# Block-sorted attention and FFN on one core: v sorted and loaded in another order, spread matrices in bf16, a third bank for the first FFN chunk

## The chip, the cores and the metric

The kernel runs on one NeuronCore of a Trainium2 chip. The engines of a core work side by side and are kept in step by semaphores: PE (TensorE, matrix products; its weight loads are shown as PEld), DVE (VectorE), ACT (ScalarE), POOL (GpSimd) and SP (SyncE). In this kernel POOL and SP do little but issue DMAs, POOL the loads that turn f32 into bf16 and SP the rest; 16 DMA engines carry them out. The metric is the time of one execution on the device in microseconds (us).

## The reference

Inputs: q, k and v of 4 batches, 8 heads, 768 positions and 64 dimensions, a sort_net of one 8x8 matrix for each batch and head, and two FFN weights (512x2048 and 2048x512) with 2048 slopes alpha.

```python
P = sort_net
for _ in range(5):                     # Sinkhorn
    P = exp(P - max(P, -1))
    P = P / (sum(P, -1) + 1e-9);  P = P / (sum(P, -2) + 1e-9)
k_sorted = einsum('bhij,bhjcd->bhicd', P, k in 8 blocks of 96)
v_sorted = einsum('bhij,bhjcd->bhicd', P, v in 8 blocks of 96)
attn = softmax(q_block @ k_sorted_block.T / 8)      # in each block of 96
x = (attn @ v_sorted_block) as (3072 tokens, 512)
h = x @ w_in
out = (max(h, 0) + alpha * min(h, 0)) @ w_out
```

So P mixes whole blocks of k and v, attention stays within a block, and each token then goes through the FFN.

## The kernel before

**Tiling.** A block of 96 positions of one batch, all 8 heads, is one step of `attention(g, ...)`; there are 32, g = 8b + i. A step is: scores (L596 for batch 0, L593 for the others), their maximum on DVE (L600), transposed scores with the maximum subtracted (L624 or L614, with L606), the exponential on ACT (L634), the product with v (L642), normalization on DVE (L647, L650), a transposition on PE (L659) and a copy into `xT` (L320, the line of all plain copies). The FFN goes over chunks of tokens, 192 for the first two and 384 for the others: `ffn1` makes 16 groups of 128 hidden rows for a chunk, each four matmuls (L679), drained by ACT (L687) and DVE (L690) into `hT`; `ffn2` makes 128 tokens of output in four parts of four matmuls (L711), and SP sends them out (L721).

**Sorting.** The sort is a product with a block-diagonal "spread" matrix, made from P on PE and DVE: `spread_k` (L446 to L454) makes BDK for a batch, `spread_v` (L461 to L469) makes BDV for two. Each starts with an f32 matmul of a selection matrix with P and ends in three DVE instructions. `prep_k` (L484) sorts k into `KT`. v of batch 0 is sorted by L526. v of the later batches is sorted by `sort_v` (L548): 12 products of 512 columns into one PSUM bank, each copied to `VD`; batch 1 is done alone, batches 2 and 3 in pairs. `turn_v` then sends `VD` to DRAM (L559) and fetches it back turned (L566), in two halves for each batch, into `VS[b % 2]`, which L642 reads. q of batches 1 to 3 is loaded in eight DMAs (L346) into `QN` and turned by six DMA transposes on SP (L353) into `QTz[b % 2]`.

**Buffers that tie steps together.** There is one `QN`, so the loads of the next q wait for the turns of the last one. `VST` has two halves: v2 goes where v0 was, and v3 where v1 was, so the load of v3 waits for the twelfth sort of v1. `KS`, `KT`, `QTz` and `VS` have two buffers each.

**Order.** Nothing is ordered by hand. Each operation is put in a graph with what it reads and writes, a duration and a priority (lower is more urgent). `schedule` simulates the five queues with its own costs (L131 to L143: for a DMA, how long it holds its issuing engine, and when it lands) and fixes each engine's order; `emit` writes this order out with the waits. An engine works strictly in that order: what stands behind a waiting instruction waits too. A priority says which of the ready operations is listed first, and the planner's costs decide what it takes to be ready. `fill` puts extra matmuls, whose result nobody reads, on PE where the planner sees it idle (L819), before the first use of their bank.

POOL's order before, behind the early loads and weights: k1, q1, k2, v1, v2, q2, q3, v3, k3. SP's order before, around q2: six turns of q2, send of half 0 of v1 (L559), an output, fetch of half 0 (L566), an output, send of half 1, fetch of half 1, then the sends of v2 and v3.

Of the kernel before, what the change touches and what calls it, by code (L numbers as in the profile page):

```python
# [7 lines left out]
AP = bass.AP  # L8
ACTF = mybir.ActivationFunctionType
BF16 = mybir.dt.bfloat16  # L10
# [46 lines left out]
class _Graph:  # L57
# [30 lines left out]
    def schedule(self):  # L88
# [31 lines left out]
        while done < len(ops):  # L120
# [14 lines left out]
            if op.dma is not None:  # L135
                free[e] = at + (600 if e == "pool" else 100)
                begin = max(dma_free if e == "pool" else 0, free[e] + 700)
                if e == "pool":
                    dma_free = begin + dur
                op.end = begin + dur + (2500 if e == "pool" else 500)  # L140
            else:
                op.end = free[e] = at + dur
# [11 lines left out]
    def fill(self, make, unit, first, before):  # L154

        out, last = [], self.ops[first].end + 300
        for op in self.order["pe"]:
            n = int((op.start - max(last, 5000)) * 0.9 / unit)
            if op.start < before and n > 0:
                x = _Op("pe", lambda e, n=n: make(e, n), n * unit, 0.0, None, len(self.ops))  # L160
                x.start, x.end = max(last, 5000), max(last, 5000) + n * unit
                x.deps.add(first)
                self.ops.append(x)
                out.append(x)
            out.append(op)
            last = max(last, op.end)
# [72 lines left out]
def bass_sinkhorn_attn__then__act_prelu_kernel(  # L239
# [29 lines left out]
    P32 = sb("P32", [32, 64], F32)  # L269
    rm = sb("rm", [32, 8], F32)  # L270
# [6 lines left out]
    selk = sb("selk", [32, 4, 128], F32)  # L277
    selv = sb("selv", [32, 2, 128], F32)
    dtmp = sb("dtmp", [128, 64], F32)
    dsel = sb("dsel", [128, 8], F32)  # L280
# [96 lines left out]
    def consts():  # L377
# [15 lines left out]
        def red(o, src, w):  # L393
# [10 lines left out]
        G.add(DVE, lambda e: e.tensor_copy(AP(VS[0], 64, [[64 * 65, 112], [65, 64]]), AP(one0, 0, [[1, 112], [0, 64]])),  # L404
              200, r=["one0"], w=[("VS1", 0)], prio=-70)
# [14 lines left out]
    def sinkhorn():  # L420
# [4 lines left out]
        for it in range(5):  # L425
# [11 lines left out]
            if it == 0:  # L437
# [3 lines left out]
            dv(lambda e: e.tensor_tensor(out=P3T, in0=P3T, in1=bc(cs), op=AluOpType.mult),  # L441
               ["P", "cs"], ["P"])

    def spread_k(b, prio):
        after = [] if b == 0 else [("xT", 1)]
        G.add(PE, lambda e: e.matmul(psYP[:, 1, 0:64], AP(selk, b * 128, [[512, 32], [1, 128]]),  # L446
                                     P32[:, :]), 500, r=["P", "selk"] + after, w=PSP, prio=prio)
        G.add(DVE, lambda e: e.tensor_tensor(
            out=AP(dtmp, 0, [[64, 128], [8, 8], [1, 8]]), in0=AP(psYP, 512, [[1024, 128], [8, 8], [1, 8]]),
            in1=AP(mkj, 0, [[8, 128], [0, 8], [1, 8]]), op=AluOpType.mult), 210,  # L450
            r=PSP + ["mkj"], w=["dtmp"], prio=prio)
        G.add(DVE, lambda e: e.reduce_sum(dsel[:, :], AP(dtmp, 0, [[64, 128], [8, 8], [1, 8]]),
                                          axis=AxisListType.X), 200, r=["dtmp"], w=["dsel"], prio=prio)
        G.add(DVE, lambda e: e.tensor_tensor(  # L454
            out=AP(BDK, b * 128, [[512, 128], [16, 8], [2, 8], [1, 2]]),
            in0=AP(mkh, 0, [[16, 128], [2, 8], [0, 8], [1, 2]]),
            in1=AP(dsel, 0, [[8, 128], [0, 8], [1, 8], [0, 2]]), op=AluOpType.mult), 260,
            r=["dsel", "mkh"], w=[("BDK", b)], prio=prio)

    def spread_v(x, prio):  # L460
        G.add(PE, lambda e: e.matmul(psYP[:, 1, 0:64], AP(selv, x * 128, [[256, 32], [1, 128]]), P32[:, :]),  # L461
              500, r=["P", "selv", ("xT", 1)], w=PSP, prio=prio)
        G.add(DVE, lambda e: e.tensor_tensor(
# [398 lines left out]
```

## Time and profile before

| | |
|---|---|
| runs, us | 303.24, 303.05, 301.84 (median 303.05) |
| the profiled execution | 301.19, with a span of 299.5 |
| PE busy from 150 us to the end | 146.35 of 149.5 us |
| loads of k, v (each, median) | 23.7 and 24.4 us from issue to landing |
| fetches of sorted v, six halves | 6.8 to 14.0 us from issue to landing |
| sends of sorted v, six halves | 3.7 to 13.3 us |
| first use of v2 and v3 on PE | 108.65 us |
| first L642 of batch 1 | 116.49 us |

The span begins with the first instruction and ends with the last; the execution's time is a little longer. In the profile's lines, L548 is a line of the kernel before. A line of the timeline is: start, duration, engine, source line, operation, what is written from what, how many; in brackets how long the engine was idle before it, and what ended that. A line of the waits is: engine and line, what it waited for, total, times, longest. PE's clock is granted by the hardware, in these rows at full or half speed.

### The profile page before, as it was taken

To read this page: it belongs to the slowest core of one execution; us is meant where nothing else is said; L and a number is where in the kernel's file an instruction comes from. 1 tells how busy PE (TensorE), PEld (TensorE's weight loads), DVE (VectorE), ACT (ScalarE), POOL (GpSimd) and SP (SyncE) were. 2 spreads that over 40 slices of the span, in tenths; PEclk is the share of its full clock that TensorE was granted. 3 is DMA by queue.
4 is the path that set the end of the run, shared out by engine and by line. 5 is a ranking of instruction groups with operands and counts; after the bars stand their busy time and mean duration, and the time that the engine had idled before them with its cause. 6 is when DMAs were issued, how large, how long until landed. Compare 5 with 4: busy or idle time off the path is not lost.

```text
span 299.5 us, 6232 instructions
## 1 busy us (share of the span) xinstructions
PE 267.3 (89%) x2705; PEld 167.4 (56%) x2705; DVE 173.2 (58%) x351; ACT 134.8 (45%) x259; POOL 35.0 (12%) x53
## 2 busy tenths in 40 slices
PE   5996999999960049999999999999999999999995
PEld 1575877663440026656666666666666666655542
DVE  6795665763760007767766666776666566654410
ACT  4384225664530016456556445434444544444421
POOL 8990000017046000000000000000000000000000
PEclk9997559999995559999999999999999999999999
DMA  6999999999899995496689940100101000100111
GB/s 121 207 206 189 215 169 214 177 166 105 129 189 88 188 191 27 125 73 155 40 131 149 64 84 35 38 2 35 37 35 37 11 27 35 37 35 35 37 70 70
DMA packets 65691, 29.78 MB, mean 99 GB/s; under 512 B 57136, under 2 KB 61248, under 8 KB 65472
## 3 DMA queue, kind: packets, MB, share of 16 engines
q0 software_dynamic: 24112, 13.63, 37.3%
q1 hardware_dynamic: 41552, 15.75, 36.6%
q8 instruction: 21, 0.34, 0.5%
q14 instruction: 6, 0.05, 0.1%
HBM read 29.64 MB, written 8.65 MB: 128 GB/s over the span
## 4 chain that ended last, share of the span: by engine, by line
PE 79%; DMA 7%; DVE 5%; SPq 2%; POOL 2%; ACT 2%; issue 1%; POOLq 0%
PE psH L679 27%; PE psYP L711 24%; DMA VST<-in_v_dram 5%; PE psS L606 4%; PE psO L642 4%; PE psS L711 3%; PE psS L593 3%; PE psS L614 3%; PE psYP L548 2%; SPq L353 2%; POOL QN L346 2%; PE psO L659 2%; PE psYP L484 2%; DMA QTz<-QN 1%; PE psS L624 1%
## 5 line engine op out<-in xcount | busy, mean ns | idle before, releaser
L690 DVE SCALAR_TENSOR_TENSOR hT<-t,omaT,psH 128x384 bf16<-128x384 f32 (+1 forms) x144 | 80.3, 566 | 79.7 <-ACT t L687 78.9
L679 PE MATMUL psH<-xT,w_in_bf 128*128 128x384 bf16 (+1 forms) x576 | 104.1, 317 | 0.6 <-DVE hT L690 0.5
L687 ACT ACTIVATE t<-psH 128x384 f32<-128x384 f32 (+1 forms) x144 | 64.6, 453 | 70.1 <-PE psH L679 69.4
L711 PE MATMUL psYP<-w_out_bf,hT 128*128 128x512 bf16 x336 | 87.0, 383 | 0.4 <-DVE hT L690 0.4
L679 PEld LDWEIGHTS psH<-xT,w_in_bf 128*128 128x128 bf16 x576 | 51.2, 101 | 28.3 <-DVE hT L690 2.7
L711 PEld LDWEIGHTS psYP<-w_out_bf,hT 128*128 128x128 bf16 x336 | 30.9, 98 | 29.0 <-issue 2.1
L634 ACT ACTIVATE Esb<-psS 96x768 bf16<-96x768 f32 (+1 forms) x31 | 25.0, 807 | 23.7 <-PE psS L606 23.1
L600 DVE TENSOR_REDUCE nm<-psS 96x8 bf16<-96x768 f32 x31 | 29.4, 950 | 2.1 <-PE psS L593 0.7
L548 PE MATMUL psYP<-VST,BDV 64*64 64x512 bf16 x36 | 9.9, 413 | 21.1 <-DMA VST<-in_v_dram 20.8
L346 POOL DMA_DIRECT2D QN<-in_q_dram x24 | 20.4, 887 | 57.6 <-DMA QTz<-QN 57.6
L606 PE MATMUL psS<-identb,nm 96*96 96x96 bf16 (+1 forms) x248 | 23.6, 215 | 0.0
L606 PEld LDWEIGHTS psS<-identb,nm 96*96 96x96 bf16 (+1 forms) x248 | 21.6, 130 | 2.3
L320 ACT ACTIVATE VD<-psYP 64x512 bf16<-64x512 f32 (+1 forms) x14 | 8.3, 594 | 30.3 <-PE psYP L548 30.1
L650 DVE TENSOR_TENSOR xq<-psO,rec 96x512 bf16<-96x512 f32 x31 | 21.3, 686 | 1.0
L642 PEld LDWEIGHTS psO<-VS,Esb 96*96 96x96 bf16 (+1 forms) x248 | 16.0, 129 | 5.7 <-ACT Esb L634 0.5
L614 PE MATMUL psS<-QTz,KT 128*96 128x192 bf16 x96 | 18.5, 248 | 0.1
L320 ACT ACTIVATE outstg<-psYP 128x512 f32<-128x512 f32 x21 | 12.5, 597 | 10.0 <-PE psYP L711 10.0
L642 PE MATMUL psO<-VS,Esb 96*96 96x65 bf16 (+1 forms) x248 | 16.7, 213 | 0.4 <-ACT Esb L634 0.2
L548 PEld LDWEIGHTS psYP<-VST,BDV 64*64 64x64 bf16 x36 | 2.5, 104 | 25.7 <-DMA VST<-in_v_dram 21.0
L819 PE MATMUL psYP<-identb 128*128 128x512 bf16 x32 | 10.5, 476 | 3.3 <-ACT identb L320 3.3
L614 PEld LDWEIGHTS psS<-QTz,KT 128*96 128x96 bf16 x96 | 11.9, 124 | 2.7 <-DVE nm L600 0.2
L593 PEld LDWEIGHTS psS<-KT,QTz 128*96 128x96 bf16 x192 | 11.5, 125 | 2.8
(112 smaller groups left out, 196.3 us busy)
## 6 DMA issues: line engine op xcount, KB each, us to landing
out_dram<-outstg SPq DMA_DIRECT2D x24, 256.0 KB, 2.0
KS<-in_k_dram POOLq DMA_DIRECT2D x4, 768.0 KB, 23.7
VST<-in_v_dram POOLq DMA_DIRECT2D x4, 768.0 KB, 24.4
QN<-in_q_dram POOLq DMA_DIRECT2D x24, 96.0 KB, 11.7
v_sorted_dram<-VD SPq DMA_DIRECT2D x6, 384.0 KB, 5.0
VS<-v_sorted_dram SPq DMA_DIRECT2D x6, 384.0 KB, 10.4
w_in_bf<-in_moe_w_in_dram POOLq DMA_DIRECT2D x4, 512.0 KB, 17.0
w_out_bf<-in_moe_w_out_dram POOLq DMA_DIRECT2D x2, 1024.0 KB, 27.3
```

The source lines that it names most:

```text
L320: return e.activation(o, i, ACTF.Copy) if e is nc.scalar else e.tensor_copy(o, i)
L346: G.add(POOL, lambda e, h=h: e.dma_start(AP(QN, h * 128 + (h // 4) * 64, [[6144, 128], [1024, 6], [1, 64]]), AP(q.tensor, b * HB + h * S * ...
L600: G.add(DVE, lambda e: e.tensor_reduce(AP(nm[m], 0, [[8, 96], [4, 2], [1, 4]]), AP(psX, 0, [[1024, 96], [512, 2], [96, 4], [1, 96]]), Axis ...
L606: return e.matmul(AP(psX, (p // 4) * 512 + (p % 4) * 96, [[1024, nk], [1, 96]]), AP(nm[m], p, [[8, 96], [0, nk]]), AP(identb, 0, [[128, 96 ...
L614: e.matmul(AP(psX, (h4 // 2) * 512 + (h4 % 2) * 192, [[1024, 96], [1, 192]]), AP(KT[n], (h4 * 8 + i) * 96, [[ld, 128], [1, 96]]), AP(QTz[n ...
L634: G.add(ACT, lambda e: e.activation(AP(Esb[m], 0, [[768, nk], [384, 2], [1, 384]]), AP(psX, 0, [[1024, nk], [512, 2], [1, 384]]), ACTF.Exp ...
L642: inst = e.matmul(AP(psZ, hp * 512 + h4 * 68, [[1024, 96], [1, 65]]), AP(Esb[m], pos(h4, hp) * 96, [[768, nk], [1, 96]]), AP(VS[n], ((hp * ...
L650: G.add(DVE, lambda e: e.tensor_tensor(out=AP(xq[m], 0, [[512, 96], [256, 2], [64, 4], [1, 64]]), in0=AP(psZ, 0, [[1024, 96], [512, 2], [6 ...
L679: inst = e.matmul(AP(psH, hb * 512, [[1024, 128], [1, n]]), AP(w_in_bf, kt * DFF + ft * 128, [[KT_TILES * DFF, 128], [1, 128]]), AP(xT, kt ...
L687: G.add(ACT, lambda e: e.activation(AP(t1[tb], 0, [[384, 128], [1, n]]), AP(psH, hb * 512, [[1024, 128], [1, n]]), ACTF.Relu, scale=-1.0), ...
L690: G.add(DVE, lambda e: e.scalar_tensor_tensor(out=AP(hT, ft * RING + tok % RING, [[FT_TILES * RING, 128], [1, n]]), in0=AP(t1[tb], 0, [[38 ...
L711: inst = e.matmul(AP(bank[0], bank[1], [[row, 128], [1, 512]]), AP(hT, ft * RING + tok % RING, [[FT_TILES * RING, 128], [1, 128]]), AP(w_o ...
```

## The change

1. The planner's DMA costs: a DMA on POOL holds it for 700 instead of 600 ns, a transposing DMA holds SP for 1300 instead of 100, and DMAs on SP of 1000 ns or more land 1000 ns later than before.
2. The sorts of v have priority 8b - 1 (they had 8b + 2 and more). For batch 1 they, and k's sorts, are listed with the last three blocks of batch 0. The load of v3 gets priority 8b - 18.5 in place of 8b - 17; q2's is 8b - 18.
3. `spread` takes the place of `spread_k` and `spread_v`. The last Sinkhorn step writes P in bf16 (`Pb`), the selection matrices are bf16, and behind batch 0's matrix the three others for k and both for v come from five matmuls into one bank, two DVE products, one reduction and four DVE products.
4. FFN1 of the first chunk (192 tokens) rotates over three PSUM banks, the third being the one that spread matrices and sorts use.
5. `fill` may also put its extra matmuls between the first FFN1 group and the first FFN2 part.
6. The ones column of `VS[0]` is copied by ACT instead of DVE, and the scores of block 2 wait for the normalization of block 1.

What this does to the queues: POOL's order becomes k1, q1, k2, v1, v2, q2, v3, first load of q3, k3, the other seven of q3. SP's order around q2 becomes: two outputs, send of half 0 of v1, a turn, an output, a turn, fetch of half 0, two turns, send of half 1, two turns, fetch of half 1, sends of v2 and v3. For q3: two turns, both fetches of v3, four turns. PE gets four filler matmuls in two pairs ahead of the first FFN2 part, and one more at the start. The twelve sorts of v1 stay spread between FFN groups, and the first sort of v2 and v3 has two more FFN1 groups ahead of it and the first scores of batch 1 behind it.

```diff
@@ schedule
-                free[e] = at + (600 if e == "pool" else 100)
+                free[e] = at + (700 if e == "pool" else 1300 if op.dur == 2500 else 100)
...
-                op.end = begin + dur + (2500 if e == "pool" else 500)
+                op.end = begin + dur + (2500 if e == "pool" else 500 if op.dur < 1000 else 1500)
@@ fill
-    def fill(self, make, unit, first, before):
+    def fill(self, make, unit, first, spans):
...
+            for lo, hi in spans:
+                begin = max(last, lo)
+                n = int((op.start - begin) * 0.9 / unit)
+                if op.start <= hi and n > 0:
...
-    G.fill(warm, 215, ident_op, first_y[0].start)
+    G.fill(warm, 215, ident_op, [(5000, first_y[0].start), (ffn_ops[0].start + 1, ffn_ops[1].start)])
@@ constants and Sinkhorn
-    selk = sb("selk", [32, 4, 128], F32)
-    selv = sb("selv", [32, 2, 128], F32)
+    selk = sb("selk", [32, 4, 128], BF16)
+    selv = sb("selv", [32, 2, 128], BF16)
...
-        G.add(DVE, lambda e: e.tensor_copy(AP(VS[0], 64, [[64 * 65, 112], [65, 64]]), AP(one0, 0, [[1, 112], [0, 64]])),
-              200, r=["one0"], w=[("VS1", 0)], prio=-70)
+        G.add(ACT, lambda e: copy(e, AP(VS[0], 64, [[64 * 65, 112], [65, 64]]), AP(one0, 0, [[1, 112], [0, 64]])),
+              220, r=["one0"], w=[("VS1", 0)], prio=-60)
...
+            o = AP(Pb, 0, [[64, 32], [1, 8], [8, 8]]) if it == 4 else P3T
+            dv(lambda e, o=o: e.tensor_tensor(out=o, in0=P3T, in1=bc(cs), op=AluOpType.mult),
+               ["P", "cs"], ["Pb" if it == 4 else "P"])
@@ spread in place of spread_k and spread_v
+    def spread(bs, vs, prio):
+        nk, nv = len(bs), len(vs)
+        after = [("xT", 1)] if vs else []
+
+        def f(e):
+            inst = None
+            for x in range(nk + nv):
+                sel = AP(selk, bs[x] * 128, [[512, 32], [1, 128]]) if x < nk else \
+                    AP(selv, vs[x - nk] * 128, [[256, 32], [1, 128]])
+                inst = e.matmul(psYP[:, 1, x * 64:x * 64 + 64], sel, Pb[:, :])
+            return inst
+        G.add(PE, f, 100 * (nk + nv), r=["Pb", "selk", "selv"] + after, w=PSP, prio=prio)
...
@@ attention
-        G.add(PE, s1, t_pe(*[(96, 96)] * 8), r=kt_keys + qt_keys, w=banks_s, prio=ps_)
+        G.add(PE, s1, t_pe(*[(96, 96)] * 8), r=kt_keys + qt_keys + [("xq", 1)] * (g == 2),
+              w=banks_s, prio=ps_)
@@ ffn1
-        hb, tb = step[0] % 2, step[0] % 3
+        tb = step[0] % 3
+        pt, poff, _, keys = (BANK_H + [BANK_P])[step[0] % 3] if ga < 2 else BANK_H[step[0] % 2]
@@ the main loop
-                load_v(3, 8 * b - 17)
+                load_v(3, 8 * b - 18.5)
...
-            for x in range(1, 4):
-                spread_k(x, x)
-                if x < 3:
-                    spread_v(x - 1, x)
+            spread([1, 2, 3], [0, 1], 1)
...
-                if i == 1 + x * 7 // len(units):
+                if i == (5 + x * 3 // len(units) if b == 0 else 1 + x * 7 // len(units)):
                     f, *a = units[x]
+                    pr = 8 * b + 2 + x * 5 / len(units)
                     if f is None:
-                        turn_v(b + 1, a[1], 8 * b + 2 + x * 5 / len(units))
+                        turn_v(b + 1, a[1], 8 * b - 1)
+                    elif f is sort_v:
+                        f(*a, 8 * b - 1)
                     else:
-                        f(*a, 8 * b + 2 + x * 5 / len(units))
+                        f(*a, pr)
```

## The prediction

> **What bounds the kernel now.** First the page's slices, for where TensorE (PE) is not full:
>
> ```profile
> span 299.5 us, 6232 instructions
> ...
> PE 267.3 (89%) x2705; PEld 167.4 (56%) x2705; DVE 173.2 (58%) x351; ACT 134.8 (45%) x259; POOL 35.0 (12%) x53
> ...
> PE   5996999999960049999999999999999999999995
> ...
> PEclk9997559999995559999999999999999999999999
> DMA  6999999999899995496689940100101000100111
> ```
>
> A slice is 7.5 us. PE is full except at the start and in slices 12 to 14, where the DMA engines are full instead. From there on PE alone sets the pace. The waits, then PE, POOL and SP in order of time, say what the hole is:
>
> ```profile
> PE psYP L548 <- DMA VST<-in_v_dram: 20.8, 1, 20.8
> ```
> ```profile
> 87.28 0.52 PE L593 MATMUL psS<-KT,QTz 128*96 128x96 bf16 x8
> 108.65 0.63 PE L548 MATMUL psYP<-VST,BDV 64*64 64x512 bf16 x2 [20.84 <-DMA VST<-in_v_dram]
> ```
> ```profile
> 66.15 6.62 POOL L346 DMA_DIRECT2D QN<-in_q_dram  x8 [43.73 <-DMA QTz<-QN]
> 86.66 6.56 POOL L346 DMA_DIRECT2D QN<-in_q_dram  x8 [13.89 <-DMA QTz<-QN]
> 93.14 0.62 POOL L371 DMA_DIRECT2D VST<-in_v_dram  x1
> ```
> ```profile
> 75.47 8.86 SPq L353 DMA_TRANSPOSE QTz<-QN  x6
> ...
> 89.05 0.34 SPq L566 DMA_DIRECT2D VS<-v_sorted_dram  x1
> ...
> 94.26 0.45 SPq L559 DMA_DIRECT2D v_sorted_dram<-VD  x1
> 107.56 0.34 SPq L566 DMA_DIRECT2D VS<-v_sorted_dram  x1
> ```
>
> (start, duration, work, idle before it.) PE stands 20.84 us at the first sort of v2 and v3, because v3 was issued only at 93.14: POOL's queue had q3 ahead of it, q3 (86.66) waited for the six turns of q2, and these (75.47) for q2's loads (66.15). Last, the granted clock by stages:
>
> ```profile
> 30.00:45.00 15.00, 15.00 (x116) 11.56 (x116) 9.74 (x30) 4.27 (x11) 0.00 (x0) 0.55 1.61 192
> ...
> 93.00:108.60 15.60, 0.00 (x0) 0.00 (x0) 0.00 (x0) 0.00 (x0) 1.34 (x3) 0.50 2.22 155
> ```
>
> The first number after the comma is PE's busy time, the third from the end the clock. It is half from 26.4 to 43.5 although PE is busy, and from 91.3 to 111.8 because of the hole.
>
> **v3's place.** In the changed program POOL has v3 behind q2 and ahead of q3 and k3 (so not ahead of q2). Its buffer half is free after the twelfth sort of v1: 76.32 before, and one FFN1 group (four 384-wide L679, 0.65) later in the new PE order: 77.0. Issue 0.6, latency about 1.3 (the 8 KB of sort_net landed 1.6 after issue), then the load: v1 and v2 landed 4.1 apart (21.35+33.2, 21.9+36.7) while turns were under way. So v3 lands at about 83. That the sorts are listed as more urgent changes little: v1 landed at 54.5, its first sort ran at 57.45, and the new order has it behind the same work. PE meets its first sort at 87.8, plus two FFN1 groups now ahead (1.3), less eight score matmuls now behind (0.45): 88.6. The 20.84 go, and with them the half clock behind the hole: eight L679 took 2.63 there and 1.41 afterwards; with the sorts about 1.5 us.
>
> **What is late next.** The first output matmul of batch 1 (L642, 116.49 before) needs both halves of v1 back from DRAM, sent and fetched by SP. Before, that wait was hidden under the hole. SP's new order is: turn, out, turn, fetch half 0, two turns, send half 1, two turns, fetch half 1, so the fetch waits behind all turns, and behind it wait SP's sends of v2 and v3. On PE everything waits behind that L642, and VectorE's (DVE) L647 with it.
>
> When does half 1 land? The first turn starts at 75.5 as before (q2 is not moved). Shortest: the DMAs only cost SP's issue time: turns 8.9, send 0.5, fetch 0.3, out 0.3 make 10.0, and v3's 4.1 on top (turns landed 12.8 us after issue among the loads of v1 and v2, 3.3 to 5.1 alone): 89.6; the fetch then takes its least, 6.8 (the one of 140.64): 96.4. Longest: everything in series, with the fetch of half 0 at 5 (6.8 less some 2 of latency) and a send at 2 (3.7 less the same): 8.9+4.1+5+2+0.5 = 20.5, so 96.0, and the fetch takes 12.4 as beside q3: 108.4. For the end of SP's turns I take the middle, 93, and for the fetch 8.8, which this very fetch took (107.56 to 116.4) beside k3: L = 102, nearer the row that had loads beside it, because q3 and k3 follow the last turn here too.
>
> The Trainium skill's "DMA: Bandwidth & Descriptors" (Issuing engines are not separate DMA queues) speaks against the change: transfers of all issuing engines run on the same 16 DMA engines and interleave, so v3 ahead takes from the turns what it gains. This trace shows both sides: turns that landed 12.8 after issue among loads, and a busy share of 0.92 in 75.5 to 80, with turns alone. By the rule everything is in series, L is 108.4 and the sum would be 290.9 in place of 284.5.
>
> PE gets to that L642 from 88.6 by seven pairs of sorts (0.34 each), two sets of scores (0.45), four FFN1 groups (0.65), two sets of transposed scores (0.8) and two FFN2 parts (0.87): 9.2, so 97.9.
>
> **Spread matrices.** Four f32 matmul pairs leave PE (0.61 each, L446 and L461 at half clock: 2.5). Five bf16 matmuls of 64 columns come: 16 of L484 take 0.37 at full clock, so 0.05 each at half, 0.3. DVE had 4x(0.22+0.22+0.29) = 2.9; it gets two products (0.22 for 64 columns, 0.69 for 512: 0.3 each), one reduction of 320 (between 0.22 for 64 and 0.95 for 768: 0.45) and four products of 0.29 to 0.4: 2.4, under PE's work in that stage (DVE busy 9.74 of 15). Without that cover FFN1's first drain would wait up to 2.4, which three banks absorb. The first spread, on the path, gains 0.2 (one pass instead of the 0.43 of two).
>
> **Three banks, fillers.** PE idles 0.0 of 30 to 45 and 0.4 of 45 to 60: the bank gains at most 0.4. Four filler matmuls (two pairs of L819) cost 0.23 each at full clock and 0.44 at half: 0.9 to 1.8. They may bring the clock back earlier. Bounds: nothing, or 8.5 if none of the 17.1 us ran at half. Nearest row: after the hole the clock was back 3.1 us after dense FFN1 work began, while in 26 to 43 small matmuls kept PE busy at half. I take 0.9, half of a 3.4 us step at half speed. The Trainium skill's "TensorE: Matmul & The Clock Gate" (Part 1) has full clock return after one busy window of about 3.4 us. This trace disagrees: 15.00 of 15 busy, clock 0.55. By the page this term is 0 and the fillers only cost: -1.2 for front and middle in place of -2.1.
>
> **Start.** A 0.64 copy (L404) leaves DVE's Sinkhorn chain for ACT, but the chain waits there for ACT's exp (ended 5.39; reduction done 5.93, own time 0.22) and another reduction of 0.27 moves into the gap: gain 0.1 to 0.3; on ACT the copy lies in 1.86 of idle time ahead of the third exp. One more filler ahead of q's transposition (0.44) delays ACT's three copies ahead of the fifth exp: loss up to 0.4. Sum -0.1. Block 2's scores now follow block 1's normalization, so DVE's 0.95 reduction (25.75) no longer delays block 0's; but PE idled only 0.5 of 26.7 to 30 and 0.0 after, so between -0.5 and +0.5: 0, hidden by PE's own work.
>
> Front and middle: -0.1-0.2-2.5+0.3+1.3-0.9 = -2.1. PE reaches the L642 at 97.9-2.1 = 95.8. This is ahead of L, so these parts only lengthen the new wait; they are worth something only where L is early.
>
> **Sum.** From 116.49 to the end of the span are 183.0, dense (PE idles 0.1 of 112 to 120, 3.2 of the last 149.5, nearly all of it the tail). The new order has done more before that point: four pairs of sorts 1.4, one set of transposed scores 0.8, one FFN1 group 0.65, one FFN2 part 0.87, in all 3.7. So the span ends at max(95.8, 102)+179.3 = 281.3. The new wait is 6 us, long enough for the clock to fall again (before: 3.5 us after PE stopped); its return cost 1.5, which I take at two chances in three: +1. Span 282.3. The profiled execution was 301.19 with a span of 299.5, so 1.7 around it: 284.0. It lies 1.86 below the median 303.05; a run without the hole should scatter less, so I add 0.5: 284.5.
>
> Later transfers: k3 is issued at about 97 and may take its old 18.9: 116, while its first use on PE, behind the last group of k2 (147.12, 30.6 behind the L642 before; less 3.7), comes near 129. v2's last half landed at 147.4 for a use at 152.04, and its sorts now come 1.4 sooner; q3's turns were done by 164 for a use past 200.
>
> **Rivals.** (1) No new wait, PE sets the point: 95.8+179.3+1.7 = 276.8 to 278.7 with scatter. For: SP's own time is 10 us. Against: fetches beside loads took 8.8 to 12.4. 0.20. (2) The hole stays in part: v3 takes its old 15.5 and lands at 93; PE idles 6 there, does 9.2 and finds L past: 102.2, then 283 to 287. Against: v1 and v2 took 4.1. 0.08. (3) The returns of v1 queue up as before (send 13.3, fetch 12.4): sent at 86, fetched from 99, landed 112: 112+179.3+1.5+1.7 = 294.5. 0.08. (4) The other side: half 1 lands after 120.2 (299.5-179.3); past 121.7 the kernel is slower, 306 at 125. One mechanism: SP's queue is in order, and turns starved by loads hold it. The turns of q1 took 19.5 (46.6 to 66.15) among three loads; here one load is beside them. 0.03. (5) No gain at all, v3 held by something unseen: 0.02.
>
> The forecast has 0.59. From rival 1 (277.5) to just short of rival 3 the range holds 8 in 10: 277.5 to 292.5, the ends that 96.4 and 108.4 give with their clock and scatter. 0.5% is about what a measurement can tell from no change. Faster 0.95, same 0.02, slower 0.03.
>
> **What would show it.** The hole at L548 gone, v3 landing at 82 to 86; a new wait of 2 to 10 us at the first L642 of batch 1, behind the fetch; the clock full again before 43.5, or not; nothing waiting after 110. It is wrong if v3's load is starved by turns, if half 1 lands past 109, or if the clock stays at half for longer after the new wait.

## The result

The kernel after takes 287.3 us (median of four runs, 286.67 to 288.38), the kernel before 303.06 in runs beside it: a ratio of 0.949 (95% interval 0.945 to 0.953), 15.8 us less by the medians. The prediction on record was 284.5, with a range of 277.5 to 292.5. The profiled execution after is the slowest of the four, 288.38 with a span of 286.7.

The page of the kernel after: where PE is not full, at which clock, and what the DMA engines do.

```profile
span 286.7 us, 6187 instructions
...
PE 261.7 (91%) x2669; PEld 163.4 (57%) x2704; DVE 173.2 (60%) x346; ACT 133.4 (47%) x256; POOL 35.4 (12%) x53
...
PE   5996999789999329999999999999999999999995
...
PEclk9997799989999957999999999999999999999999
DMA  6999999999999999994699800010001110100111
```

In place of the three slices with 0, 0 and 4 tenths, two are left, the fourteenth and fifteenth, with 3 and 2. PE's waits (total, times, longest) and its rows in order of time (start, duration, work, in brackets the idle time before) say what is left:

```profile
PE psO L651 <- DMA VS<-v_sorted_dram: 9.4, 1, 9.4
...
PE psYP L556 <- DMA VST<-in_v_dram: 1.8, 1, 1.8
```

```profile
54.74 0.40 PE L556 MATMUL psYP<-VST,BDV 64*64 64x512 bf16 x1 [1.83 <-DMA VST<-in_v_dram]
...
85.89 0.40 PE L556 MATMUL psYP<-VST,BDV 64*64 64x512 bf16 x2
...
95.61 0.40 PE L556 MATMUL psYP<-VST,BDV 64*64 64x512 bf16 x2
...
105.46 0.85 PE L651 MATMUL psO<-VS,Esb 96*96 96x65 bf16 x8 [9.45 <-DMA VS<-v_sorted_dram]
```

PE reaches the first sort of v2 and v3 (L556, which was L548) at 85.89 and doesn't wait there. It comes to the first output product of batch 1 (L651, which was L642) at 96.0 and stands 9.45 us for the second half of v1 to come back from DRAM. A second, smaller wait is new: 1.83 at the first sort of v1, because PE gets there sooner. POOL's and SP's rows of the kernel after give the two chains:

```profile
66.06 6.63 POOL L349 DMA_DIRECT2D QN<-in_q_dram  x8 [43.38 <-DMA QTz<-QN]
75.09 0.54 POOL L374 DMA_DIRECT2D VST<-in_v_dram  x1 [2.39 <-PE psYP L556]
100.95 0.85 POOL L349 DMA_DIRECT2D QN<-in_q_dram  x1 [25.32 <-DMA QTz<-QN]
```
```profile
75.66 1.24 SPq L356 DMA_TRANSPOSE QTz<-QN  x1
...
77.70 5.21 SPq L356 DMA_TRANSPOSE QTz<-QN  x1
82.97 0.59 SPq L574 DMA_DIRECT2D VS<-v_sorted_dram  x1
83.60 9.48 SPq L356 DMA_TRANSPOSE QTz<-QN  x2
93.13 0.59 SPq L567 DMA_DIRECT2D v_sorted_dram<-VD  x1
93.76 4.29 SPq L356 DMA_TRANSPOSE QTz<-QN  x2
98.10 0.61 SPq L574 DMA_DIRECT2D VS<-v_sorted_dram  x1
```

v3 is issued at 75.09, ahead of q3, and lands 7.9 us later, at 83.0. On SP the six turns (L356) stand between the pieces of v1's return; the fetch of half 1 (L574) goes out at 98.10 and lands at 105.42. From there PE is dense to the end, as before.

### The profile page after: what moved, and what is told of

Its sections match the earlier page's. It is cut to its first block, busy times and chain, and to the rows that moved or that the text cites. A ratio compares the mean times of both kernels' runs of the same rounds, so it can differ in the third digit from the quotient of the medians.

```text
span 286.7 us, 6187 instructions
## 1 busy us (share of the span) xinstructions
PE 261.7 (91%) x2669; PEld 163.4 (57%) x2704; DVE 173.2 (60%) x346; ACT 133.4 (47%) x256; POOL 35.4 (12%) x53
## 4 chain that ended last, share of the span: by engine, by line
PE 68%; DMA 14%; SPq 7%; POOL 7%; issue 2%; DVE 1%; ACT 0%; POOLq 0%
PE psH L690 24%; PE psYP L724 23%; DMA VST<-in_v_dram 12%; SPq L356 7%; PE psS L724 4%; PE psO L651 3%; PE psS L615 3%; PE psS L601 3%; PE psS L623 3%; DMA VS<-v_sorted_dram 3%; POOL QN L349 2%; PE psYP L556 2%; PE psYP L492 2%; PE psO L668 2%; POOL QN L391 1%
## 5 line engine op out<-in xcount | busy, mean ns | idle before, releaser
L703 DVE SCALAR_TENSOR_TENSOR hT<-t,omaT,psH 128x384 bf16<-128x384 f32 (+1 forms) x139 | 78.4, 571 | 52.4 <-ACT t L700 51.7
L690 PE MATMUL psH<-xT,w_in_bf 128*128 128x384 bf16 (+1 forms) x556 | 100.7, 314 | 0.7 <-DVE hT L703 0.7
L700 ACT ACTIVATE t<-psH 128x384 f32<-128x384 f32 (+1 forms) x139 | 63.5, 458 | 66.3 <-PE psH L690 65.1
L724 PE MATMUL psYP<-w_out_bf,hT 128*128 128x512 bf16 x302 | 81.1, 386 | 3.1 <-issue 1.0
L690 PEld LDWEIGHTS psH<-xT,w_in_bf 128*128 128x128 bf16 x556 | 48.5, 99 | 26.2 <-DVE hT L703 2.8
L349 POOL DMA_DIRECT2D QN<-in_q_dram x24 | 21.0, 911 | 68.7 <-DMA QTz<-QN 68.7
L651 PE MATMUL psO<-VS,Esb 96*96 96x65 bf16 (+1 forms) x248 | 16.4, 211 | 9.5 <-DMA VS<-v_sorted_dram 9.4
L651 PEld LDWEIGHTS psO<-VS,Esb 96*96 96x96 bf16 (+1 forms) x248 | 15.9, 127 | 15.4 <-DMA VS<-v_sorted_dram 9.7
L623 PE MATMUL psS<-QTz,KT 128*96 128x192 bf16 x96 | 18.5, 249 | 0.2 <-DVE nm L609 0.2
L656 DVE RECIPROCAL rec<-psO 96x8 f32<-96x8 f32 x31 | 6.3, 202 | 18.6 <-PE psO L651 18.0
L323 ACT ACTIVATE outstg<-psYP 128x512 f32<-128x512 f32 x21 | 12.5, 597 | 9.7 <-PE psYP L724 9.7
L323 ACT ACTIVATE VD<-psYP 64x512 bf16<-64x512 f32 (+1 forms) x11 | 6.5, 593 | 21.2 <-PE psYP L556 21.1
L323 DVE CAST VD<-psYP 128x512 bf16<-128x512 f32 (+1 forms) x13 | 9.0, 691 | 12.0 <-PE psYP L556 9.4
L834 PE MATMUL psYP<-identb 128*128 128x512 bf16 x37 | 12.3, 476 | 3.3 <-ACT identb L323 3.3
## 6 DMA issues: line engine op xcount, KB each, us to landing
KS<-in_k_dram POOLq DMA_DIRECT2D x4, 768.0 KB, 20.5
QN<-in_q_dram POOLq DMA_DIRECT2D x24, 96.0 KB, 17.3
w_in_bf<-in_moe_w_in_dram POOLq DMA_DIRECT2D x4, 512.0 KB, 17.1
```

The source lines that it names most:

```text
L323: return e.activation(o, i, ACTF.Copy) if e is nc.scalar else e.tensor_copy(o, i)
L349: G.add(POOL, lambda e, h=h: e.dma_start(AP(QN, h * 128 + (h // 4) * 64, [[6144, 128], [1024, 6], [1, 64]]), AP(q.tensor, b * HB + h * S * ...
L623: e.matmul(AP(psX, (h4 // 2) * 512 + (h4 % 2) * 192, [[1024, 96], [1, 192]]), AP(KT[n], (h4 * 8 + i) * 96, [[ld, 128], [1, 96]]), AP(QTz[n ...
L651: inst = e.matmul(AP(psZ, hp * 512 + h4 * 68, [[1024, 96], [1, 65]]), AP(Esb[m], pos(h4, hp) * 96, [[768, nk], [1, 96]]), AP(VS[n], ((hp * ...
L690: inst = e.matmul(AP(pt, poff, [[1024, 128], [1, n]]), AP(w_in_bf, kt * DFF + ft * 128, [[KT_TILES * DFF, 128], [1, 128]]), AP(xT, kt * XR ...
L700: G.add(ACT, lambda e: e.activation(AP(t1[tb], 0, [[384, 128], [1, n]]), AP(pt, poff, [[1024, 128], [1, n]]), ACTF.Relu, scale=-1.0), t_ac ...
```

## The experiments

The theory: the planner's new DMA costs alone remove the hole, by putting v3 ahead of q3; the new wait comes from the turns on SP between the sends and fetches of v1. The rivals: spread matrices, third bank and fillers carry the gain, or the fetch would be late without the turns too. Every ratio below is to runs of the kernel before on the same chip.

### The two halves of the change

With only the new priority of v3 taken back, the order on every engine stays that of the kernel after; so the priority was left with the costs. First the kernel after with the old planner costs:

```diff
-                free[e] = at + (700 if e == "pool" else 1300 if op.dur == 2500 else 100)
+                free[e] = at + (600 if e == "pool" else 100)
...
-                op.end = begin + dur + (2500 if e == "pool" else 500 if op.dur < 1000 else 1500)
+                op.end = begin + dur + (2500 if e == "pool" else 500)
...
-                load_v(3, 8 * b - 18.5)
+                load_v(3, 8 * b - 17)
```

> The changed kernel with the planner's old DMA costs and v3's old priority: seven of q3's eight loads stand ahead of v3 again. Theory: PE stands about 20 us at the first sort of v2 and v3, until 107 to 109, the first L651 of batch 1 waits for nothing, and the time is 299 to 302 us: the parts without v3's place are worth 1 to 4 us of the 15.8. Rival (the spread matrices, the banks and the fillers carry a large part themselves): 290 to 297.

Measured: 299.79 us, ratio 0.991 (0.988 to 0.994). Its PE and POOL rows:

```profile
108.95 0.63 PE L556 MATMUL psYP<-VST,BDV 64*64 64x512 bf16 x2 [24.14 <-issue]
```
```profile
89.84 5.74 POOL L349 DMA_DIRECT2D QN<-in_q_dram  x7 [17.04 <-DMA QTz<-QN]
95.53 0.60 POOL L374 DMA_DIRECT2D VST<-in_v_dram  x1
```

v3 stands behind seven loads of q3 again and the hole is back, 24.14 us long: PE gets there sooner and waits longer. The other way round, the new costs and the new priority put into the kernel before, with nothing else (there too the priority changes no engine's order, so it is the costs that act):

> The kernel before, with the planner's new DMA costs and the new priority of v3's load alone: v3 stands ahead of q3 in POOL's queue, the fetch of half 1 of v1 behind the turns of q2 on SP; f32 spreads, two banks and no new fillers as before. Theory (v3's place is nearly all of the gain, and the fetch of half 1, at about 105, sets the point from which PE runs on, so that what the start of the kernel gains is lost in the wait): the hole at L548 gone, a wait of 6 to 10 us at the first L642 of batch 1, the clock at half from 26 to 43 as before, 287 to 291 us. Rival (the denser start is worth its 2 to 3 us at the end): 290 to 293 with a shorter wait at that L642, of 3 to 6 us.

Measured: 292.86 us, ratio 0.968 (0.965 to 0.970). No hole at the sort; at the first output product of batch 1:

```profile
106.25 0.85 PE L642 MATMUL psO<-VS,Esb 96*96 96x65 bf16 x8 [11.11 <-DMA VS<-v_sorted_dram]
```

That is 2 us over the theory's range. The time lies in the rival's range, but its mechanism, a wait of 3 to 6 us, did not come: the wait is 11.11, longer than either said. So the costs alone are worth 9.8 us and everything else alone 2.9; together they give 15.8. The rest is worth 5.6 with the costs in place, although PE still waits for half 1 of v1 in both kernels. The two traces say where 4.0 of it lies: half 1 lands 0.8 sooner, and from the first output product of batch 1 to the end the kernel after takes 181.2 us where this one takes 184.4. Of these 3.2, the clock accounts for about 1.3 (full again 5.5 us after PE resumes instead of 8.0); the rest is work that the kernel after has done ahead of the wait, three pairs of sorts and an FFN2 part.

### The turns

The kernel after, with the turns of q2 waiting until the send of half 1 has landed, so that the planner lists them behind the fetch:

```diff
-            2500, r=[("QN", h) for h in range(H)],
+            2500, r=[("QN", h) for h in range(H)] + [("scr", 1, 1)] * (b == 2),
```

> The changed kernel, but the turns of q2 also wait until half 1 of v1 has been sent, so that SP's order is send, fetch, send, fetch, and then the six turns. Theory (the new wait at the first L651 of batch 1 comes from SP's queue order, where the fetch of half 1 stands behind turns that are slowed by loads and by the fetch of half 0): half 1 lands between 88 and 94, PE gets to that L651 at about 95 without a wait over 1 us, the clock stays full there, and the span is 275 to 278: 277 to 280 us, some 9 less than the changed kernel. Rival A (the DMA engines are the limit, whatever the order: v3, the sends and the fetches take until 100 in any case): a wait of 5 us or more stays, 283 to 287. Rival B (the wait moves on to the turns of q2, which now end later, at the first scores of batch 2, or to k3): no wait at batch 1, but a new one behind 120, 282 to 288.

Measured: 281.67 us (six runs, 279.43 to 283.91), ratio 0.929 (0.925 to 0.933): 5.6 us better than the kernel after. The median is 1.7 over the range expected, while two of the six, 279.43 and 279.63, lie in it. The rows below are of the one at 283.91: in it the clock was at half for 20.5 us in three stretches, where the mean clock of those two, 0.982, makes 10. They show where such an execution loses. SP's rows, then PE's:

```profile
68.04 0.52 SPq L567 DMA_DIRECT2D v_sorted_dram<-VD  x1
...
74.52 0.42 SPq L574 DMA_DIRECT2D VS<-v_sorted_dram  x1
77.80 2.44 SPq L567 DMA_DIRECT2D v_sorted_dram<-VD  x1
92.23 0.34 SPq L574 DMA_DIRECT2D VS<-v_sorted_dram  x1
```
```profile
55.55 0.40 PE L556 MATMUL psYP<-VST,BDV 64*64 64x512 bf16 x1 [2.56 <-DMA VST<-in_v_dram]
...
91.59 0.64 PE L556 MATMUL psYP<-VST,BDV 64*64 64x512 bf16 x2 [2.51 <-issue]
...
102.18 0.55 PE L651 MATMUL psO<-VS,Esb 96*96 96x65 bf16 x8
```

The wait of 9.45 us is gone, for two reasons. The fetch of half 1 goes out 5.9 us sooner and lands at 99.6 instead of 105.4; that much of the wait the turns did cause. And PE comes to the product only at 102.2 instead of 96.0, after the two waits and the half clock behind them; had it come at 96.0, it would have waited 3.6. The fetch doesn't gain the whole time that the turns had held SP, because the send of half 1 now takes 14.4 us (4.6 in the kernel after). v3 takes 14.2 instead of 7.9, lands at 91.5 and PE waits for it. So a part of the rival holds too: without the turns half 1 is still late.

### Fillers, bf16 and the third bank

Three single reversals in the kernel after. Without the fillers behind the first FFN1 group:

```diff
-    G.fill(warm, 215, ident_op, [(5000, first_y[0].start), (ffn_ops[0].start + 1, ffn_ops[1].start)])
+    G.fill(warm, 215, ident_op, [(5000, first_y[0].start)])
```

> The changed kernel without the four filler matmuls in front of the first FFN2 part. Theory (PE's pace before 96 us is lost in the wait at the first L651 of batch 1): within 1 us of the changed kernel's 287.3, whatever the clock does. On the clock: if the fillers bring it back, it returns later than 32.4 (at 36 to 43) and PE reaches the first sort of v2 and v3 1 to 3 us later than 85.9; if the one-go spread and the other order bring it back, it returns at 32 to 36 here too. Rival: PE's pace counts at the end, 289 to 291 us.

With f32 spread products again (every engine's order unchanged):

```diff
-    Pb = sb("Pb", [32, 64], BF16)
+    Pb = sb("Pb", [32, 64], F32)
...
-    selk = sb("selk", [32, 4, 128], BF16)
-    selv = sb("selv", [32, 2, 128], BF16)
+    selk = sb("selk", [32, 4, 128], F32)
+    selv = sb("selv", [32, 2, 128], F32)
```

> The kernel after with P, the selection matrices and so the five spread products in f32 again; the order on every engine is that of the kernel after, so nothing but these five products differs. Theory 1 (the f32 products hold PE's clock back): the half clock that begins at 25.6 lasts 10 us or more in place of 6.8. Theory 2 (it is how full PE is, whatever it multiplies): 6.8 us again. The five products themselves cost five times 0.42 less 0.23, so 0.9 us, ahead of the wait at the first product with sorted v of batch 1, which takes it up: 287 to 288 by theory 2, at most 288 by theory 1, and the wait is shorter by what PE loses.

With two banks for the first chunk:

```diff
-        pt, poff, _, keys = (BANK_H + [BANK_P])[step[0] % 3] if ga < 2 else BANK_H[step[0] % 2]
+        pt, poff, _, keys = BANK_H[step[0] % 2]
```

> The kernel after with two banks for the first FFN chunk, as in the kernel before; the planner then puts more extra matmuls there and moves work. Theory: the third bank keeps PE fed ahead of 43 us; without it PE reaches the first sort of v1 later by up to 2 us and waits less there for v1, and the wait for the second half of v1 takes up what is left: 286 to 289. If the third bank is what brings the clock back at 32.4, the half clock lasts 10 us or more here; if it isn't, 6.8. Rival: the order that it moves changes the place of the returns of v1 among the turns, and the time moves by more than 2 us either way.

Measured: 287.34 (four runs, ratio 0.951, 0.948 to 0.955), then 286.28 and 289.74 (a single run each). PE's wait at L651 was 10.86, 8.91 and 10.31: what PE gains or loses ahead is mostly taken up there, as expected. The two banks' run is 0.7 over its range: its wait ends at 104.64, and from there it takes 183.4 us instead of 181.2, with the clock back 7.5 us after PE resumed instead of 5.5, and a pair of sorts and an FFN2 part more still to do. The first long stretch at half clock, by the profile's record of the granted clock:

```
kernel                        half clock from, us     for, us
before                        26.4                    17.1
new costs only                25.5                    17.1
after                         25.6                     6.8
after, old costs              24.3                    10.2
after, no fillers             24.4                    10.2
after, f32 spread             25.9                    10.2
after, two banks              26.8                     6.8
```

By its letter the f32 run fits theory 1, but so would the run without fillers, where nothing is f32. No single part brings the clock back: each reversal leaves 6.8 or 10.2, a step of 3.4 apart, which is also how far kernels with the same order up to there differ (the run with v3 told late, below, has 10.2, the one with the turns alone 6.8). All kernels with the new front have 10.2 or less and both with the old one 17.1.

What fits all fourteen traces is how much PE streams, not how long it is busy. Cut each stretch into steps of 3.41 us from the fall of the clock, and add up for each step the columns that its products stream, each weighted by the rows and columns of the array that the product uses (1 for 128*128; as some records are missing, the sums are a little low):

```
step                           1      2      3      4      5
before                      1757   2485   1864   1821   3704
new costs only              1668   2053   2312   1941   2816
after                       1712   3400
after, no fillers           1330   2480   3029
after, f32 spread            928   1641   3252
```

The clock is full again behind the last step of each row. In this first stretch every step with 2485 or less, over all the traces, left it at half, and every one with 2816 or more brought it back, though PE isn't idle at all in steps 3 and 4 of the kernel before. There the spread products in f32 stand one or two to a step until 40.0, and each keeps PE busy for 0.6 us; in the kernel after all five stand in step 1. No run varied this alone, and in later stretches the two ranges overlap (3264 left it at half, 2416 brought it back), so this account fits the front but isn't shown to be the cause.

### What is left behind the turns

Six kernels started from the turns' edit or its idea, to remove the two waits of 2.5 us. First v1 ahead of k2 on POOL, alone and with v3's load told to the planner as 4000 ns longer:

```diff
-               load_us, w=[("KS", b % 2)], prio=prio, dma=(d_k[b % 2], 0))
+               load_us, r=[("cv", u) for u in range(4)] * (b == 2), w=[("KS", b % 2)], prio=prio, dma=(d_k[b % 2], 0))
...
-              r=[("VST", 0), ("VST", 1)], w=[("VD", u)], prio=prio)
+              r=[("VST", 0), ("VST", 1)], w=[("VD", u), ("cv", u)], prio=prio)
```

> The kernel after with the turns of q2 behind the send of half 1 of v1 (as in the run before it, 281.67 median) and, beside that, the load of v1 put ahead of the load of k2 on POOL: k2's load now also waits for the four conversions of v0 that v1's load waits for, so the two are equally ready and priority decides. In the run without it k2 landed before v1 and PE waited 2.56 us for v1 at its first sort (55.55); the clock then fell to half for 6.8 us, which costs 3.4 us. Theory (the late v1 is a cost of its own): v1 lands about 3.4 us earlier, both go, the time is 275.7, between 274 and 279. The wait of about 2.5 us at the first sort of v2 and v3 stays, since v3 still follows the twelfth sort of v1, and may grow by as much as PE arrives earlier. Rival (one chain of DMAs sets the time: v3's landing, sends and fetches are late whatever PE does earlier): what is gained ahead is waited for at the first sort of v2 and v3, and the time stays at 281 to 282.

> As the run beside it (turns behind the send of half 1, v1 ahead of k2), and the planner is told that v3's load takes 4000 ns more, so it lists one block's scores and transposed scores and an FFN group ahead of the first sort of v2 and v3, where PE waited 2.5 us. Theory: work that is there fills that wait and the half clock of 6.8 us behind it does not come, together up to 5.9 us: 270 to 276 where the run beside it is 275.7. Rival (the work put ahead is only taken from behind, where PE then waits for the sorts, the sends or the fetches of v2): no gain on the run beside it, and a new wait at the first product with sorted v of batch 2.

Measured: 288.54 (ratio 0.952, 0.945 to 0.958) and 286.2 (0.947, 0.942 to 0.951): 6.9 and 4.5 us worse than with the turns alone, so worse than theory and rival both. POOL's and PE's rows of the first:

```profile
21.20 0.54 POOL L374 DMA_DIRECT2D VST<-in_v_dram  x1 [0.83 <-DVE VD L323]
21.73 0.58 POOL L364 DMA_DIRECT2D KS<-in_k_dram  x1
```
```profile
55.15 0.63 PE L556 MATMUL psYP<-VST,BDV 64*64 64x512 bf16 x1 [5.11 <-DMA VST<-in_v_dram]
...
95.00 0.63 PE L556 MATMUL psYP<-VST,BDV 64*64 64x512 bf16 x2 [7.31 <-issue]
```

v1, though issued first, is there at 55.1, when it was there behind k2 (55.5); in the second of the two it landed at 54.2. So its place among three loads issued within 1.1 us doesn't set its landing. The planner, which counted on an earlier v1, put less work ahead of its sort, so PE waited 5.11 instead of 2.56, and more again at v3. Next, the loads left alone and only the planner told that they take longer, so that other work stands ahead of the sorts: v3 by 6000 ns, then v3 by 6000 and v1 by 4000.

```diff
-            load_us, w=[("VST", b % 2)], prio=prio, dma=(d_v[b], 0))
+            load_us + {1: 4000, 3: 6000}.get(b, 0), w=[("VST", b % 2)], prio=prio, dma=(d_v[b], 0))
```

> The kernel after with the turns of q2 behind the send of half 1 (281.67 median), and the planner told that v3's load takes 6000 ns more; v1 stays behind k2. The order is the same up to the first sort of v2 and v3, ahead of which stand now a block's scores, its transposed scores and two FFN groups more. Theory (two waits of 2.5 us, each followed by 6.8 us of half clock worth 3.4, are what is left to gain): the wait at the first sort of v2 and v3 goes and so does the half clock behind it, the one at v1 (2.6) stays: 276 to 279. Rival (what fills the wait is only taken from behind, where PE waits for the sends and fetches of v2): 281 to 284.

> As the run beside it, and the planner also told that v1's load takes 4000 ns more: one block's work and four FFN groups stand ahead of the first sort of v1, where PE waited 2.6 us, and the sorts, the send and the fetches of v1 are listed that much later. Theory: both waits and both half clocks go, 271 to 276. Rival (v1's chain is what bounds batch 1: sorts begun later mean the second half lands later and PE waits at the first product with it again): a wait at that product of 1 to 5 us and 277 to 283.

Measured: 281.44 and 281.35 (ratios 0.931, both 0.924 to 0.938). PE's first output product of batch 1, in the one and in the other:

```profile
97.59 0.69 PE L651 MATMUL psO<-VS,Esb 96*96 96x65 bf16 x8 [2.10 <-DMA VS<-v_sorted_dram]
```
```profile
98.51 0.55 PE L651 MATMUL psO<-VS,Esb 96*96 96x65 bf16 x8 [3.28 <-DMA VS<-v_sorted_dram]
```

The waits at the sorts go (in the second both), and the time stays: PE waits for half 1 of v1 instead. That is the second run's rival, number and mechanism; the first run's time is its rival's too, but that rival had named v2's sends and fetches. v1's return bounds this stage. So why do send, load and fetch take 12 to 14 us there? First suspect: the loads of q2, held back until the send has landed, in the kernel after:

```diff
-                load_us / 8, r=[("QN0", h)], w=[("QN", h)], prio=prio, dma=(d_qn[h], 0))
+                load_us / 8, r=[("QN0", h)] + [("scr", 1, 1)] * (b == 2), w=[("QN", h)], prio=prio, dma=(d_qn[h], 0))
```

> The kernel after with one edit: the eight loads of q2 wait until the send of half 1 of v1 has landed, so v3's load stands ahead of all of q2 on POOL, and the turns of q2, which wait for the loads, come behind the fetch of half 1. Unlike the run that only held the turns back (281.67 median), nothing of q2 is under way while fetch of half 0, send of half 1 and the load of v3 are; there these took 13.4, 14.4 and 14.2 us from issue to landing, alone some 7, 4 and 8. Theory (they were late because q2's loads, 12 to 20 us from issue to landing, shared the DMA engines with them): v3 lands 4 to 6 us earlier, ahead of its first sort, the second half of v1 lands by 94, and no wait is left but the 2.6 us for v1: 281.7 less 2.5 and less 3.4 of half clock, 275.8, between 274 and 279. Rival 1 (the three are slow because of each other, not of q2's loads): their landings stay at 12 us and more and the time at 281 to 283. Rival 2 (the turns of q2, later by 10 us, now hold SP when the sorted v2 is to be sent and fetched): the first product with sorted v of batch 2 waits, and the time is 283 or more.

Measured: 281.65 (ratio 0.929, 0.922 to 0.936). With nothing of q2 under way, v3 still took 12.8, the send 12.5 and the fetch of half 0 10.9 (14.2, 14.4 and 13.4 in the run with the turns alone): rival 1, though q2 had some part in it. Half 1 of v1 did land at 94.3, as the theory had it, and PE didn't wait for it. But the wait at v3's sort stays and, a part of rival 2, one comes at 138.64:

```profile
86.53 0.40 PE L556 MATMUL psYP<-VST,BDV 64*64 64x512 bf16 x2 [1.98 <-issue]
...
138.64 0.52 PE L651 MATMUL psO<-VS,Esb 96*96 96x65 bf16 x8 [2.18 <-issue]
```

Second suspect: the fetch of half 0 is issued too late, behind an output, and so meets v3. A shorter send in the planner (with the turns' edit) puts it ahead of that output:

```diff
-              4000, r=[("VN", c, b % 2) for c in range(6 * x, 6 * x + 6)], w=[("scr", b, x)], prio=prio,
+              3000, r=[("VN", c, b % 2) for c in range(6 * x, 6 * x + 6)], w=[("scr", b, x)], prio=prio,
```

> The kernel after with the turns of q2 behind the send of half 1 (281.67 median), and the planner told that a send takes 3000 instead of 4000 ns, which puts the fetch of half 0 ahead of the output on SP that it stood behind (74.13, waiting for its data, with the send landed at about 71.6), and the first product with sorted v of batch 1 one FFN group earlier. In the trace of that kernel the fetch's 128-byte packets ran at some 780 to 1050 in a microsecond while they were alone and at 340 to 400 beside v3's 12 KB ones, and the packets of send 1, on the same queue, began only when the fetch was through, at 86. Theory (fetch of half 0 is late by the output, and so collides with v3 and blocks send 1): issued at 70 to 72 it is through by 78, v3 lands by 86 and send 1 by 84, the wait of 2.5 us at the first sort of v2 and v3 and its half clock go, fetch 1 lands by 94: 276 to 278. Rival (q2's loads, which are then under way, or the send itself hold the fetch just as long, or PE waits for half 1 instead): v3 lands at 90 or later, or a wait of over 2 us at the first product with sorted v of batch 1, and 280 to 283.

Measured: 283.06 (six runs, ratio 0.935, 0.930 to 0.940). The fetch went out at 69.11, 5.4 us sooner, and landed 12.4 later all the same; v3 took 13.2 and the send of half 1 13.5:

```profile
88.08 0.40 PE L556 MATMUL psYP<-VST,BDV 64*64 64x512 bf16 x2 [2.42 <-issue]
...
98.15 0.85 PE L651 MATMUL psO<-VS,Esb 96*96 96x65 bf16 x8 [2.62 <-DMA VS<-v_sorted_dram]
```

The rival again. What the suspects had in common was the fetch of half 0. Where a half was fetched by itself, half 0 took 9.5 to 17.3 us from issue to landing in the fourteen traces, half 1 6.7 to 10.2, but for two that ran beside v3's and k3's loads (13.4 and 18.4). The packets in the trace of the kernel after, counted by the microsecond in which they start, while v3 was already there:

```
us           84    85    86    87    88    89    90    91
128 B       301   856   409   397   402   359   317    24
median ns    13    13    69    69    69    82    66    65
256 B       879                                44   227
```

After some 1,000 of its 3,072 packets the fetch falls from 13 ns a packet to about 70 and stays there for five microseconds, with no other data on record from 85 to 90. The fetch of half 1 of v2 in the kernel before does the same with its second half, but at 36 to 44 ns. It isn't v3 that slows it: in the run with the turns alone it is slow from 79 on, and v3's first 12 KB packet starts at 82.6. The turns (256 B) that SP issued behind it move next to nothing until it is through; nor does, in the run with the turns alone, the send of half 1, whose first packets come at 86. And v3's load, on POOL's queue, is held as well: with q2 held back its first 12 KB packet starts 4.5 us after issue (1.25 in the kernel after), when the fetch is nearly through, and the 15 that still run beside the fetch take 2.4 us each, the others 0.93. So by the traces it is the slow second part of the fetch of half 0 that holds the queues in this stage; no run changed the fetch itself, so this is read and not shown by an experiment. Why its packets are slow, and nearly twice as slow as those of half 1, is open. Writing it to fewer or other partitions at a time was not tried.

So the turns behind the fetch, 281.67, are better than both kernels; the four others at 281.35 to 283.06 can't be told from it, as their intervals overlap with its own.

## Why the prediction was right, point by point

- **The hole.** Right: v3 ahead of q3 removes it, and the costs alone do it.
- **v3 lands at 83.** Measured 83.0, by two errors that cancel: issued at 75.09 instead of 77.0, and 7.9 under way instead of 6.0.
- **PE at the first sort of v2 and v3 at 86.5, at the output product at 95.8.** Measured 85.89 and 96.0. That both came so near is partly luck, as the make-up was off. Five f32 pairs left PE and not four, 3.1 us instead of 2.5. The clock term of 0.9 was too small: half clock lasted 6.8 us instead of 17.1, worth up to 5. And the text did not see what was late next there: v1, at 54.5 before, with some 3 us to spare; PE now got there at 52.9, waited 1.83 and then ran at half clock for 3.4 us (56.3 to 59.7), which costs 1.7.
- **What is late next: half 1 of v1, at 102 within 96.4 to 108.4.** Right in kind, and 105.42 lies within. The step that was mis-sized is the end of SP's turns: taken as 93, and at most 96.0 "everything in series"; measured 98.06. That upper bound counted the fetch of half 0 with 5 us of data, less than the 6.8 of a fetch of half 1 by some 2 of latency; it took 10.8 in all. The six turns held SP for 20.2 us where they had held it 8.9: 3.5 more for the two beside v3's load, near the 4.1 counted, 1.3 for the last two, and 6.5 for the two behind the fetch of half 0, whose 9.48 stand in the rows above. The last fetch took 7.3 instead of 8.8. In the prediction's own rows the fetch of half 0 stood with 12.4; one figure for both halves was the error.
- **The Trainium skill's "DMA: Bandwidth & Descriptors" (Issuing engines are not separate DMA queues).** The page says that transfers of all issuing engines share the 16 DMA engines and interleave; the prediction took that as all in series, with half 1 due at 108.4, and 105.42 is nearer to that than to 102. The run with q2 held back agrees: v3 on POOL's queue took 12.8 beside SP's fetch and send, 7.9 where its packets were through before the fetch began.
- **The new wait of 6.** Measured 9.45: L is 3.4 later and PE arrives at 96.0. The clock fell again, at 100.7, and came back only at 110.95, 5.5 us after PE resumed, which costs 2.7 instead of the 1 counted.
- **The rest.** From L651 to the end 181.2, where 179.3 + 1 was said. The span is 4.4 longer than the 282.3 predicted: 3.4 from L, 1.7 from the clock, less 0.7 of the rest.
- **Nothing waits after 110.** Right: k3 and q3, issued 8 to 15 us later, cost nothing.

Rival 1 (no new wait) was excluded by the trace of the kernel after, rival 2 by v3's landing. Rival 3 and the slower one named the right place, SP's ordered queue. That the last fetch went out at 98.1, near rival 3's 99, is chance: rival 3 had it behind a send of 13.3 us, and the send took 4.6 and was itself late by the turns. Its 112 failed because the last fetch took 7.3 and not 12.4. And what held the turns was the fetch ahead of them more than a load, 6.5 us against 3.5.

## What to carry to other kernels

When a hole goes, price the next wait by the queue that serves it, piece by piece, and give each transfer the duration of its own kind: here two fetches of equal size, 10.8 and 7.3 us, differ by a half. A planner that believes a transfer lands early moves PE's work away from in front of it; telling it a later time moved the waits, but only reordering the queue that was the bound (turns behind the fetch) moved the time. Time that PE gains ahead of a wait is waited away there, as with the fillers; what still counts is work moved from behind the wait to ahead of it, and how soon the clock is full again. So measure parts together as well as alone. And before reading the rows of one profiled run as the kernel's, see where its time stands among the runs.

## What the runs showed of the hardware

- A fetch of 128-byte packets runs in two gaits: 13 ns a packet for the first 1,000 to 1,200, then 65 to 82 (half 0) or 36 to 44 (half 1) where nothing else is under way, in the kernel before as after.
- With three loads of 768 KB issued within 1.4 us, v1 landed at 55.1 and 54.2 when issued ahead of k2, and at 54.4 to 55.5 behind it in the other twelve traces: its place didn't matter to it. k2 did lose, 57.6 to 59.1 instead of 50.8 to 52.2.
- Each stretch at half clock that ends inside a span lasts a whole number of steps of 3.41 us, from one to seven. Much of the spread between runs of one kernel goes with such steps: with the turns behind the fetch, the mean clock is 0.982 where the time is 279.4 and 279.6, some three steps at half, and 0.962 where it is 283.9, some six.
- The clock stayed at half for 17.1 us with the old front, with PE at 4.00 us busy in each 4 from 32 to 40, and for 6.8 to 10.2 with the new one. The Trainium skill's "TensorE: Matmul & The Clock Gate" (Part 1) gives one busy window of about 3.4 us for the return. The kernel after agrees: PE idles 0.84 us in the step from 25.6 and not at all in the one from 29.0, and the clock is full from 32.4 on. The kernel before doesn't, if busy is what the profile shows: three steps with less than 0.1 us of idle time each went by at half clock, until 40.0, and only the next one ended it. Rows of the kernel before, then of the kernel after (window, length, then PE's busy time; the clock is third from the end):

```profile
36.00:40.00 4.00, 4.00 (x23) 3.01 (x22) 2.23 (x9) 1.17 (x4) 0.00 (x0) 0.50 1.22 199
```
```profile
28.00:32.00 4.00, 4.00 (x34) 3.23 (x35) 3.15 (x9) 1.47 (x4) 0.00 (x0) 0.50 1.23 200
32.00:36.00 4.00, 3.95 (x43) 2.71 (x42) 2.94 (x7) 2.03 (x6) 0.00 (x0) 0.94 1.26 214
```
